# Token and channel mixer: the products of chunks 16 to 54 as two lanes of 64 rows, each in its own order

## The chip, the core and the metric

One Trainium2 chip, one core. The metric is device microseconds of one execution. Engines in the views: PE is TensorE's matmuls, PEld its weight loads, DVE is VectorE, ACT is ScalarE, POOL is GpSimd, SP is SyncE.

## What is computed

```python
w = softmax(weight_gen)                      # (8, 4096, 8 heads, 7 taps), over the taps
x = causal_taps(w, x)                        # out[s] = sum_k w[s,k] * x[s-6+k], per head; (8, 4096, 192)
xt = x.transpose(0, 2, 1)
h = np.maximum(xt @ w_tok1, 0.0) @ w_tok2    # 4096 -> 256 -> 4096: over the sequence
u = x + h.transpose(0, 2, 1)
h2 = np.maximum(u @ w_ch1, 0.0) @ w_ch2      # 192 -> 1536 -> 192: over the channels
return u + h2
```

## The kernel before

The 8 x 4096 positions are 64 chunks of 512 (`NG` = 64, `NCH` = 8 a batch). Each operand of a product is held as a high and a low part, and a product is taken as two or three products of parts. Per chunk `g` the kernel does:

- the attention of a later chunk: tap products and sums on DVE (L278, L292), added into `xa` by DMA, cut into `xh` (L329 on ACT, L332 on DVE), turned and kept (L354), with a softmax for two chunks at a time (L237 to L246);
- token 1 of a later chunk (L600, L602): 8 pairs of products, 384 and 192 columns, into `th`, which ACT seeds from `h1s` (L593) and copies back (L610). From batch 2 on (chunk 16) in parts;
- token 2 of chunk `g + 1` (L643): ten products of 512 columns into `up`, a two-bank PSUM tile that ACT first seeds with a copy of `xb` (L637). Then `uf` (L650 to L655) and its parts `u_hi`, `u_lo` (L678 to L693), here the "u chain";
- channel 1 (L749): six pairs `p` of hidden blocks, each nine steps of two products; the two use rows 0 to 63 and 64 to 127 of PE and write the two banks of one tile `ph`. Then `h`: its high part is ACT's ReLU (L755), its low part DVE's difference (L756). Four `h` are kept (`HB` = 4), so pairs 4 and 5 stay in PSUM until channel 2 has used up a buffer;
- channel 2 (L767): 60 products of full height (128 rows) into two banks `acc`, seeded from `uf` (L816); then `store` (L825 to L847) transposes them on DVE, ACT copies them to `out_tile`, SP stores.

PSUM has eight banks: two for `acc`, three two-bank tiles (tag `w`, a ring in order of use) for `ph`, `up` and `th`. Each engine works through its own list in order. The lists are written in the program's order; where work of the attention, the u chain and the stores stands in DVE's and ACT's lists is chosen by `pump` from planned times (`at`, `on`). PE's list before is plain: channel 1's 108 products, token 2's ten, half of channel 2, token 1, the other half of channel 2.

Of the kernel before, what the change touches and what calls it, by code (L numbers as in the profile page):

```python
# [22 lines left out]
def mixer_kernel(ctx: ExitStack, tc: tile.TileContext, x, wg, wt1, wt2, wc1, wc2, out):  # L23
# [558 lines left out]

    def token1(m):
        b, i = divmod(m, NCH)
        w = w1t.pop(m)
        th = ps_w.tile([P, 2, 512], F32, tag="w", name="th")
        cols = slice(0, D if b < F1 else 2 * D)
        if i == 0:  # L590
            h1s[b] = late.tile([P, KR, 2 * D], F32, tag="h1s", name="h1s")[:, :, cols]
        else:
            nc.scalar.copy(th[:, :, cols], h1s[b])  # L593
        yield
        if b >= F1:
            xh = xht.pop(m)
            for r in range(KR):
                for c in range(CT):
                    rs = slice(r * P, (r + 1) * P)
                    nc.tensor.matmul(th[:, r, 0:2 * D], w[:, c, 0, rs], xh[:, c, :], start=i + c == 0, stop=False,  # L600
                                     skip_group_check=True)
                    nc.tensor.matmul(th[:, r, 0:D], w[:, c, 1, rs], xh[:, c, 0:D], start=False, stop=c == CT - 1,  # L602
                                     skip_group_check=True)
# [19 lines left out]

    ut, uft = {}, {}

    def token2(m, up=None):

        xb, h1, w = xbt.pop(m), h1t[m // NCH], w2t.pop(m)
        seeded = up is None
        if seeded:  # L630
            up = ps_w.tile([P, 2, 512], F32, tag="w", name="up")
            if m < 2:
                nc.scalar.copy(up, xb)
            elif m < FT:
# [104 lines left out]
    def channel1(g, p):  # L739

        u_hi, u_lo = ut[g]
        ph = ps_w.tile([P, 2, 512], F32, tag="w", name="ph")
        steps = [(w, u, k) for w, u in ((w1_hi, u_hi), (w1_lo, u_hi), (w1_hi, u_lo)) for k in range(3)]
        if g == 0:
            steps = [(w, u_hi, k) for k in (2, 0, 1) for w in (w1_hi, w1_lo)] + [(w1_hi, u_lo, k) for k in (0, 2, 1)]
        for n, (w, u, k) in enumerate(steps):
            for j in range(2):
                rows = slice(j * DC, (j + 1) * DC)
                nc.tensor.matmul(ph[:, j, :], w[rows, k, p * P:(p + 1) * P], u[rows, k], start=n == 0,  # L749
                                 stop=n == len(steps) - 1)  # L750
# [9 lines left out]
    def channel2(g, p):  # L760
        acc = acc_t[g]
        h = ht.pop((g, p))
        for j in range(2):
            f = 2 * p + j
            for n, steps in ((1, ((C_HL, 0), (C_HL, 1))), (0, ((A_HI, 0), (A_LO, 0), (A_HI, 1)))):
                for i, (d, l) in enumerate(steps):
                    nc.tensor.matmul(acc[n], w2s[:, f, d], h[:, j, l, :], start=False,  # L767
                                     stop=f == NF - 1 and i == len(steps) - 1, skip_group_check=True)

    def last_chunk(g, p0):  # L770

# [114 lines left out]
    def on(engine, cost, *after):  # L886
        at[engine] = max(at[engine], *after, 0.0) + cost
        return at[engine] + HOP

    class Chain:  # L890
# [4 lines left out]
        def next(self):  # L895
            self.item = next(self.items, None)
# [77 lines left out]

# [64 lines left out]
    with tc.tile_pool(name="pro", bufs=1) as pro, \  # L1039
# [353 lines left out]
```

## Time and profile before

| | us |
|---|---|
| median of 3 runs (2054.68 to 2054.95) | 2054.75 |
| span of the profiled execution, first to last instruction | 2052.6 |
| PE busy in the span | 2031.9 (99%) |
| DVE busy | 1498.8 (73%) |
| ACT busy | 1436.9 (70%) |
| stretch of chunks 16 to 54 (39 chunks) | 585.5 to 1790.0 |

The span is one execution; the runs' times hold 2.15 us outside of it. A matmul's end is modelled (its row is longer than the step from start to start), so the pace of PE is read from the starts.

### The profile page before, as it was taken

How to read it: one execution, taken by the hardware profiler on the slowest of the kernel's cores; microseconds unless marked ns; L12 is line 12 of the kernel's file. 1: busy time of each engine (PE TensorE's matmuls, PEld its weight loads, DVE VectorE, ACT ScalarE, POOL GpSimd, SP SyncE). 2: the span in 40 equal slices, each digit the busy share in tenths (PEclk: the TensorE clock that was granted, in tenths of full speed). 3: DMA queues.
4: the chain of work that ended last, by engine and by line, in shares of the span. 5: the costliest groups of instructions: out<-in, count | busy, mean ns of one | idle time of the engine just before them, and what ended most of it. 6: DMA issues, size and time to landing. Idle time of an engine off the chain costs nothing.

```text
span 2052.6 us, 32256 instructions
## 1 busy us (share of the span) xinstructions
PE 2031.9 (99%) x12831; PEld 1675.4 (82%) x12831; DVE 1498.8 (73%) x1735; ACT 1436.9 (70%) x2282; POOL 210.2 (10%) x292
## 2 busy tenths in 40 slices
PE   7999999999999999999999999999999999999999
PEld 7878888888888888888888888888888888888887
DVE  9899988888987778767777768768678774434343
ACT  7887667677776676676676676676676676676665
POOL 1101111111111101001101111001111010000000
PEclk9999999999999999999999999999999999999999
DMA  9978778887886676666666676766676662222121
GB/s 336 282 226 227 201 212 226 217 223 206 245 212 179 169 192 184 176 201 157 186 197 163 174 200 166 200 177 166 177 200 168 177 181 82 90 73 64 45 65 24
DMA packets 180898, 361.47 MB, mean 176 GB/s; under 512 B 26138, under 2 KB 129178, under 8 KB 165004
## 3 DMA queue, kind: packets, MB, share of 16 engines
q1 hardware_dynamic: 145420, 225.35, 35.5%
q0 software_dynamic: 35328, 134.07, 27.7%
q8 instruction: 100, 1.64, 0.3%
q14 instruction: 50, 0.41, 0.1%
HBM read 222.77 MB, written 70.52 MB: 143 GB/s over the span
## 4 chain that ended last, share of the span: by engine, by line
PE 97%; DVE 2%; ACT 1%; issue 0%; DMA 0%; ACTq 0%; DVEq 0%
PE acc L767 41%; PE ph L749 39%; PE up L643 8%; PE th L600 4%; PE th L602 2%; PE th L621 2%; DVE prk L404 1%; PE up L767 1%; PE tapsum L414 1%; PE acc L786 0%; DVE val L202 0%; PE up L724 0%; PE acc_end L786 0%; ACT few L206 0%; PE turn L414 0%
## 5 line engine op out<-in xcount | busy, mean ns | idle before, releaser
L767 PE MATMUL acc<-h,w2s 128*128 128x512 f32 x3740 | 870.3, 390 | 0.0
L767 PEld LDWEIGHTS acc<-h,w2s 128*128 128x128 f32 x3740 | 698.0, 188 | 143.3 <-issue 0.7
L755 ACT ACTIVATE h<-ph 128x1024 fp32r<-128x1024 f32 x384 | 394.2, 1026 | 365.5 <-PE ph L749 324.6
L756 DVE SCALAR_TENSOR_TENSOR h<-ph,h 128x1024 fp32r<-128x1024 f32 x384 | 467.1, 1218 | 103.8 <-ACT h L755 102.6
L749 PE MATMUL ph<-u_hi,w_hi 64*128 64x512 f32 x2304 | 334.0, 393 | 0.0
L749 PE MATMUL ph<-u_hi,w_lo 64*128 64x512 f32 x2304 | 326.4, 386 | 0.0
L749 PE MATMUL ph<-u_lo,w_hi 64*128 64x512 f32 x2304 | 325.0, 387 | 0.0
L278 DVE TENSOR_TENSOR pr<-xc,wg 128x768 f32<-128x768 f32 x336 | 313.0, 948 | 0.6
L296 POOL DMA_DIRECT2D xa<-pr x168 | 146.5, 872 | 1356.1 <-DVE pr L292 888.5
L749 PEld LDWEIGHTS ph<-u_hi,w_hi 64*128 64x128 f32 x2304 | 211.2, 184 | 63.8 <-issue 20.1
L749 PEld LDWEIGHTS ph<-u_hi,w_lo 64*128 64x128 f32 x2304 | 215.9, 184 | 46.7
L749 PEld LDWEIGHTS ph<-u_lo,w_hi 64*128 64x128 f32 x2304 | 215.9, 184 | 46.4 <-ACT u_lo L737 0.3
L835 ACT COPY out_tile<-oa 32x256 f32<-32x256 f32 x504 | 203.5, 404 | 8.2
L332 DVE TENSOR_TENSOR xh<-xa,xh 128x768 fp32r<-128x768 f32 x48 | 45.8, 955 | 179.3 <-ACT xh L329 179.1
L292 DVE TENSOR_TENSOR pr<-pr 128x768 f32<-128x768 f32 x168 | 159.9, 952 | 3.1
L643 PE MATMUL up<-w,h 128*128 128x512 f32 x630 | 161.2, 402 | 0.0
L655 DVE TENSOR_TENSOR uf<-up,uf 64x512 f32<-64x512 f32 x63 | 43.0, 683 | 145.3 <-ACT uf L651 145.3
L643 PEld LDWEIGHTS up<-w,h 128*128 128x128 f32 x630 | 114.1, 188 | 41.2 <-issue 16.9
L600 PE MATMUL th<-xh,w 128*128 128x384 f32 x384 | 112.4, 358 | 0.0
L835 ACT COPY out_tile<-oc 32x256 f32<-32x256 f32 x252 | 101.6, 403 | 4.5
L637 ACT COPY up<-xb 128x1024 f32<-128x1024 f32 x56 | 57.0, 1018 | 63.4 <-DVE h L756 63.4
L602 PE MATMUL th<-xh,w 128*128 128x192 f32 x384 | 96.2, 250 | 0.0
(115 smaller groups left out, 1728.1 us busy)
## 6 DMA issues: line engine op xcount, KB each, us to landing
w<-s SPq DMA_DIRECT2D x96, 1024.0 KB, 5.8
xa<-pr POOLq DMA_DIRECT2D x168, 384.0 KB, 4.6
xc<-in_x_dram POOLq DMA_DIRECT2D x42, 960.0 KB, 6.8
out_dram<-out_tile SPq DMA_DIRECT2D x128, 192.0 KB, 4.2
xb<-xs SPq DMA_DIRECT2D x348, 64.0 KB, 5.5
xs<-t SPq DMA_DIRECT2D x56, 384.0 KB, 5.4
raw<-in_moe_w_tok_dram SPq DMA_DIRECT2D x16, 1024.0 KB, 8.1
xc<-in_x_dram POOLq DMA_DIRECT2D x12, 840.0 KB, 7.7
```

The costliest lines, as they stand in the source:

```text
L278: nc.vector.tensor_mul(t.rearrange("p t (h g) -> p (t h) g", h=H).rearrange("p (o n) g -> p o n g", o=1), x_k, w)
L292: nc.vector.tensor_add(tap_sums[m], tap_sums[m], tap_prs.pop(m))
L296: nc.gpsimd.dma_start(xat[m].rearrange("p t d -> p (t d)"), tap_sums[m].rearrange("p t d -> p (t d)"), accum_op=ALU.add)
L600: nc.tensor.matmul(th[:, r, 0:2 * D], w[:, c, 0, rs], xh[:, c, :], start=i + c == 0, stop=False, skip_group_check=True)
L602: nc.tensor.matmul(th[:, r, 0:D], w[:, c, 1, rs], xh[:, c, 0:D], start=False, stop=c == CT - 1, skip_group_check=True)
L637: nc.scalar.copy(up.rearrange("p k (n b c) -> p (k n) c b", c=W, b=Q), xb.rearrange("p k (n c b) -> p (k n) c b", c=W, b=Q))
L643: nc.tensor.matmul(up[:, n, :], h1[:, k, d], w[:, l, k * N:(k + 1) * N], start=k == 0 and j == 0 and not seeded, stop=k == KR - 1 and j == ...
L749: nc.tensor.matmul(ph[:, j, :], w[rows, k, p * P:(p + 1) * P], u[rows, k], start=n == 0, stop=n == len(steps) - 1)
L755: nc.scalar.activation(h[:, :, 0, :], ph, AF.Relu)
L756: nc.vector.scalar_tensor_tensor(h[:, :, 1, :], ph, 0.0, h[:, :, 0, :].bitcast(F32), op0=ALU.max, op1=ALU.subtract)
L767: nc.tensor.matmul(acc[n], w2s[:, f, d], h[:, j, l, :], start=False, stop=f == NF - 1 and i == len(steps) - 1, skip_group_check=True)
L835: nc.scalar.copy(dst, src[to:to + Q].rearrange("p (n e d) -> p n e d", n=2, d=Q)[:, n])
```

## The change

From chunk 16 to 54 every product of PE is cut into two of 64 rows: lane 0 has rows 0 to 63, lane 1 rows 64 to 127. Each lane has a list of its own, and `run_lanes` merges the two into PE's one list by planned starts (a slot of 226.7 ns; 170 and 108 for token 1's halves). The two lanes don't write one bank at a time: while lane 0 sums its half of `acc[0]`, lane 1 sums its half of `acc[1]`, and then they swap. A bank goes over by an empty step on DVE or ACT (a `nop`) that waits for the last product of the one lane and for which the first of the other waits. All six `h` of a chunk are taken at once: pairs 4 and 5 into four spare tiles, one block at a time (`take_h_apart`). Token 2 and token 1 move behind the start of channel 2. Chunk 16 holds two token-1 products, and chunk 55, which had one, none; otherwise the program outside of these chunks is as before. A lane's list in a chunk is: lane 0 `ph` (54), `acc[0]` (36), `up` (10), `acc[1]` (24), `th` (8 pairs); lane 1 `ph` (54), `acc[1]` (4), `up` (10), `acc[1]` (20), `th` (8 pairs), `acc[0]` (36).

```diff
+    SLOT, T1_HI, T1_LO = 226.7, 170.0, 108.0
@@ token1 (token2 likewise, with up[:, n, :] and SLOT)
+        if lists is not None:
+            xh = xht.pop(m)
+            for s, rows in enumerate(HALVES):
+                for r in range(KR):
+                    for c in range(CT):
+                        rs = slice(r * P, (r + 1) * P)
+                        lists[s] += [
+                            (T1_HI, ("th", r, m), product(th[:, r, 0:2 * D], w[rows, c, 0, rs], xh[rows, c, :],
+                                                       s == first and i + c == 0)),
+                            (T1_LO, ("th", r, m), product(th[:, r, 0:D], w[rows, c, 1, rs], xh[rows, c, 0:D],
+                                                       stop=c == CT - 1))]
...
+    def take_h_apart(g, p, ph):
+
+        for j in range(2):
+            h = spare[(p - HB) * 2 + j]
+            nc.scalar.activation(h[:, 0, :], ph[:, j, :], AF.Relu)
+            nc.vector.scalar_tensor_tensor(
+                h[:, 1, :], ph[:, j, :], 0.0, h[:, 0, :].bitcast(F32), op0=ALU.max, op1=ALU.subtract
+            )
...
+    def run_lanes(until):
+
+        while True:
+            starts = [lane_start(s) for s in range(2)]
+            if until():
+                return
+            s = min((t, s) for s, t in enumerate(starts) if t is not None)[1]
+            cost, bank, fn = lanes[s].popleft()
+            ins = fn()
+            lane_at[s] = starts[s] + cost
+            if bank is not None:
+                if owner.setdefault(bank, s) != s:
+                    if bank in turn:
+                        behind(ins, turn.pop(bank)[0])
+                        owner[bank] = s
+                else:
+                    count[bank] = count.get(bank, 0) + 1
+                    if count[bank] == ITEMS[bank[:2]]:
+                        by, eng = min((("dve", nc.vector), ("act", nc.scalar)), key=lambda x: at[x[0]])
+                        relay = eng.nop(nofuse=True)
+                        behind(relay, ins)
+                        turn[bank] = relay, on(by, 60, lane_at[s] + HOP)
...
+        def take(p):
+            end = lane_at[1] + HOP
+            (take_h if p < HB else take_h_apart)(g, p, phs.pop(p))
+            extra = 0 if p < HB else 200
+            w_at.append(on("dve", LOW + extra, on("act", TOP + extra, end)))
+            if p == HB - 2:
+                seed(g)
...
+            if p == NP - 2:
+                begin()
...
+        def begin():
...
+            box["two"] = token2(g + 1, lists=box["t2"])
+            next(box["two"])
+            box["two_at"] = max(on("act", 1050, w_at.popleft()), h1_at[(g + 1) // NCH])
...
+            elif box["late"]:
+                upper = a + u + [hook(end_two), *c, late[0], hook(lambda: end_one("late"))]
+                lower = lc[:4] + lu + lc[4:14] + [hook(lambda: seed_late(1))] + lc[14:] + [late[1]] + la
...
+    def in_lanes(g):
+
+        return 2 * NCH <= g < NG - NCH - 1 and (ring or state["token1"] >= g + NCH - 1 and state["done"] > g + NCH)
```

In the changed kernel all products of the lanes carry one line, L469 (`product`), and the tiles of the ring are called `w`. The other lines move: the ReLU of a whole pair L755 is L799, its low part L756 is L800, ReLU and low part of one block are L792 and L793, the copy into `up` L637 is L664, the copies of `out_tile` L835 are L897, the `acc` seeds L816 are L878.

PE's list at the end of channel 1, before: the last steps of `ph`, token 2, the first of channel 2.

```order
L749 MATMUL ph<-u_hi,w_hi 128x512 x5
L749 MATMUL ph<-u_hi,w_lo 128x512 x6
L749 MATMUL ph<-u_lo,w_hi 128x512 x6
L643 MATMUL up<-w_7383,h_5848 128x512 [waits DMAHW0_49,Activation_49]
L643 MATMUL up<-w_7383,h_5848 128x512 x9
L767 MATMUL acc_7589<-h,w2s 128x512 x2
L767 MATMUL acc_7588<-h,w2s 128x512 x3
```

The same place in chunk 24 of the changed kernel. Here `w_5981` is `ph` of the last pair (lane 1), `acc0` is lane 0, `acc1` lane 1, and `w_5982` is `up` (lane 1).

```order
L469 MATMUL w_5981<-u_lo_9048,w1_hi_71 128x512
L469 MATMUL acc0_9256<-h_9202,w2s_73 128x512
L469 MATMUL acc1_9257<-h_9202,w2s_73 128x512 [waits Activation_49]
L469 MATMUL acc0_9256<-h_9227,w2s_73 128x512
L469 MATMUL acc1_9257<-h_9202,w2s_73 128x512
L469 MATMUL acc0_9256<-h_9227,w2s_73 128x512
L469 MATMUL acc1_9257<-h_9202,w2s_73 128x512
L469 MATMUL acc0_9256<-h_9227,w2s_73 128x512
L469 MATMUL acc1_9257<-h_9202,w2s_73 128x512
L469 MATMUL acc0_9256<-h_9227,w2s_73 128x512
L469 MATMUL w_5982<-w2_9049,h1_8770 128x512 [waits DMAHW7_49,DVE_49,Activation_49]
L469 MATMUL acc0_9256<-h_9227,w2s_73 128x512
```

Token 2 stood directly behind channel 1 at full height; now its first product, in lane 1, stands four products of `acc1` behind the lane's last `ph`, alternating with lane 0's `acc0`, which began six products earlier.

ACT's list from the third ReLU of a chunk to the copy into `up`, before:

```order
L755 ACTIVATE h<-ph 128x2x512 [waits PE_49]
L816 COPY acc_11876<-uf 128x512
L816 COPY acc_11877<-uf 128x512
L755 ACTIVATE h<-ph 128x2x512 [waits PE_49,Activation_49]
L637 COPY up<-xb 128x4x8x32 [waits DMAHW2_49,DMAHW3_49,DMAHW1_49,DMAHW4_49,DMAHW0_49,DVE_49]
L835 COPY out_tile<-oa 32x8x32 x2
```

The same stretch in chunk 24 of the changed kernel:

```order
L799 ACTIVATE h<-w 128x2x512 [waits PE_49]
L878 COPY acc_9256<-uf 128x512
L878 COPY acc_9257<-uf 128x512
L799 ACTIVATE h<-w 128x2x512 [waits DVE_49,PE_49]
L792 ACTIVATE h_spare<-w 128x512 [waits DVE_49,PE_49]
L792 ACTIVATE h_spare<-w 128x512 [waits DVE_49]
L664 COPY w<-xb 128x4x8x32 [waits DMAHW5_49,DMAHW6_49,DMAHW2_49,DMAHW7_49,DMAHW1_49,DMAHW0_49]
L792 ACTIVATE h_spare<-w 128x512 [waits PE_49]
L792 ACTIVATE h_spare<-w 128x512 [waits DVE_49]
```

The copy into `up` (`L664`) stood behind the fourth ReLU; now the two ReLUs of the fifth pair stand between, and the second of them waits for the count that DVE's low part of the first block (L793) brings.

DVE's list in chunk 24 of the changed kernel, from the sum of `oc` to the low parts of the fifth pair:

```order
L890 TENSOR_TENSOR oc<-oc 64x512 [waits DVE_49]
L240 TENSOR_REDUCE mx<-wg 128x64 [waits Activation_49]
L800 SCALAR_TENSOR_TENSOR h<-w,h 128x2x512 [waits Activation_49]
L243 TENSOR_SCALAR mx<-mx 128x64 [waits DVE_49]
L244 RECIPROCAL mx<-mx 128x64 [waits DVE_49]
L800 SCALAR_TENSOR_TENSOR h<-w,h 128x2x512 [waits Activation_49]
L246 TENSOR_TENSOR wg<-wg,mx 128x448 [waits DVE_49]
L800 SCALAR_TENSOR_TENSOR h<-w,h 128x2x512 [waits Activation_49]
L278 TENSOR_TENSOR pr<-xc,wg 128x768
L800 SCALAR_TENSOR_TENSOR h<-w,h 128x2x512 [waits Activation_49]
L354 STREAM_TRANSPOSE t<-xa 128x768 [waits DMAHW6_49,DMASW0_49]
L793 SCALAR_TENSOR_TENSOR h_spare<-w,h_spare 128x512 [waits Activation_49] x2
```

Ahead of these rows stand the two transposes of the chunk before and `xh` (L887, L888, L332). One operation of the attention stands between the fourth low part and the first of the fifth pair in chunks 17 to 51 (in odd chunks L292). The softmax rows (L240 to L246) are in the even chunks 18 to 48.

## Rows read from the trace of the kernel before

**Rows 1.** The head of the page: the span.

```profile
span 2052.6 us, 32256 instructions
```

**Rows 2.** Who PE waited for in the whole span: engine, its line, the releaser; us in total, times, longest.

```profile
PE tapsum L414 <- DVE prk L404: 13.1, 5, 9.1
PE th L621 <- ACT xa L461: 2.2, 3, 0.9
PE up L767 <- DVE w2s L561: 0.3, 1, 0.3
```

**Rows 3.** Busy time in the stretch of chunks 16 to 54: us; PE, PEld, DVE, ACT, POOL busy (instructions), granted clock, DMA share, GB/s.

```profile
585.50:1790.00 1204.50, 1204.50 (x7567) 989.63 (x7566) 871.55 (x1022) 835.15 (x1342) 126.64 (x169) 1.00 0.64 174
```

**Rows 4.** Timeline of PE in chunk 30 and the ends of its neighbours: start, us to the end of the last of them, line, operation, count.

```profile
1015.76 2.20 PE L767 MATMUL acc<-h,w2s 128*128 128x512 f32 x9
1017.89 0.97 PE L749 MATMUL ph<-u_hi,w_hi 64*128 64x512 f32 x6
...
1020.09 0.85 PE L749 MATMUL ph<-u_hi,w_hi 64*128 64x512 f32 x6
...
1026.21 0.84 PE L749 MATMUL ph<-u_hi,w_hi 64*128 64x512 f32 x6
...
1029.61 0.84 PE L749 MATMUL ph<-u_lo,w_hi 64*128 64x512 f32 x6
1030.38 2.58 PE L643 MATMUL up<-w,h 128*128 128x512 f32 x10
1032.80 6.96 PE L767 MATMUL acc<-h,w2s 128*128 128x512 f32 x30
1039.60 0.33 PE L600 MATMUL th<-xh,w 128*128 128x384 f32 x1
...
1039.86 0.36 PE L600 MATMUL th<-xh,w 128*128 128x384 f32 x1
1040.06 0.25 PE L602 MATMUL th<-xh,w 128*128 128x192 f32 x1
1040.15 0.36 PE L600 MATMUL th<-xh,w 128*128 128x384 f32 x1
```

**Rows 5.** Timeline of PE in chunk 55, where token 2 stands between the halves of channel 2.

```profile
1804.87 7.00 PE L767 MATMUL acc<-h,w2s 128*128 128x512 f32 x30
1811.70 2.43 PE L643 MATMUL up<-w,h 128*128 128x512 f32 x10
1813.97 6.96 PE L767 MATMUL acc<-h,w2s 128*128 128x512 f32 x30
```

**Rows 6.** Timeline of DVE in channel 1 of chunk 30; in brackets the idle time ahead and what ended it.

```profile
1018.00 0.72 DVE L825 STREAM_TRANSPOSE oa<-acc 128x512 f32<-128x512 f32 x1
1018.64 0.67 DVE L826 STREAM_TRANSPOSE oc<-acc 128x512 f32<-128x512 f32 x1
1019.35 0.69 DVE L828 TENSOR_TENSOR oc<-oc 64x512 f32<-64x512 f32 x1
1020.07 0.96 DVE L292 TENSOR_TENSOR pr<-pr 128x768 f32<-128x768 f32 x1
1020.95 0.61 DVE L237 TENSOR_REDUCE mx<-wg 128x64 f32<-128x448 f32 x1
1021.48 1.22 DVE L756 SCALAR_TENSOR_TENSOR h<-ph,h 128x1024 fp32r<-128x1024 f32 x1
...
1027.53 1.22 DVE L756 SCALAR_TENSOR_TENSOR h<-ph,h 128x1024 fp32r<-128x1024 f32 x1 [0.31 <-ACT h L755]
1028.67 0.95 DVE L292 TENSOR_TENSOR pr<-pr 128x768 f32<-128x768 f32 x1
1029.54 1.82 DVE L278 TENSOR_TENSOR pr<-xc,wg 128x768 f32<-128x768 f32 x2
```

**Rows 7.** Timeline of ACT in the same stretch: the first ReLU and the copy into `up`.

```profile
1020.29 1.03 ACT L755 ACTIVATE h<-ph 128x1024 fp32r<-128x1024 f32 x1 [5.93 <-PE ph L749]
...
1028.79 1.02 ACT L637 COPY up<-xb 128x1024 f32<-128x1024 f32 x1 [1.29 <-DVE h L756]
```

**Rows 8.** Groups of ACT by line and shape, 580 to 1728 us: count | busy us, mean ns of one | idle us before.

```profile
L755 ACT ACTIVATE h<-ph 128x1024 fp32r<-128x1024 f32 x222 | 227.9, 1027 | 217.7 <-PE ph L749 194.7 <-PE acc L767 22.1
...
L637 ACT COPY up<-xb 128x1024 f32<-128x1024 f32 x37 | 37.6, 1017 | 44.1 <-DVE h L756 44.1
...
L593 ACT COPY th<-h1s 128x768 f32<-128x768 f32 x32 | 25.7, 802 | 5.4 <-DVE h L756 5.2
...
L691 ACT CAST u_hi<-uf 64x512 fp32r<-64x512 f32 x38 | 23.5, 619 | 0.6
...
L651 ACT COPY uf<-up 128x512 f32<-128x512 f32 x38 | 22.3, 587 | 0.4
```

**Rows 9.** Groups of DVE by line and shape, the same stretch.

```profile
L756 DVE SCALAR_TENSOR_TENSOR h<-ph,h 128x1024 fp32r<-128x1024 f32 x222 | 269.9, 1218 | 30.0 <-ACT h L755 29.0
...
L681 DVE TENSOR_TENSOR u_lo<-uf,u_hi 128x512 fp32r<-128x512 f32 x38 | 25.7, 676 | 0.0
```

**Rows 10.** Timeline around the one wait of PE behind 100 us: DVE's operation that it waited for, PE's first product after it, and the next products.

```profile
111.84 0.43 DVE L561 TENSOR_TENSOR w2s<-val,w2s 128x256 fp32r<-128x256 f32 x1
112.32 0.72 PE L767 MATMUL up<-h,w2s 128*128 128x512 f32 x2 [0.26 <-DVE w2s L561]
112.66 0.86 PE L767 MATMUL up<-h,w2s 128*128 128x512 f32 x3
```

More of the change, by code (lines that the diff above doesn't have):

```diff
@@ L461, in turn_back, with product, w_tile @@
         nc.scalar.copy(new_xa(m).rearrange("p c d -> p (c d)"), ps[:, 0:NB * P])
+    HALVES = (LO, HI)
+    SLOT, T1_HI, T1_LO = 226.7, 170.0, 108.0
+    def product(to, w, v, start=False, stop=False):
+        return lambda: nc.tensor.matmul(to, w, v, start=start, stop=stop, skip_group_check=True)
+    ring = deque()
+    def w_tile(name):
+        if not ring:
+            return ps_w.tile([P, 2, 512], F32, tag="w", name=name)
+        ring.rotate(-1)
+        return ring[-1]
     w1t, w2t, rawt = {}, {}, {}
@@ L580, in make_h1, with token1 @@
                                            op0=ALU.max, op1=ALU.subtract)
-    def token1(m):
+    def token1(m, lists=None, first=1):
         b, i = divmod(m, NCH)
         w = w1t.pop(m)
-        th = ps_w.tile([P, 2, 512], F32, tag="w", name="th")
+        th = w_tile("th")
         cols = slice(0, D if b < F1 else 2 * D)
@@ L594, in token1 @@
         yield
-        if b >= F1:
+        if lists is not None:
[9 more added lines that the diff above has]
+                                                       stop=c == CT - 1))]
+        elif b >= F1:
             xh = xht.pop(m)
@@ L624, in mixer_kernel, with token2 @@
     ut, uft = {}, {}
-    def token2(m, up=None):
+    def token2(m, up=None, lists=None):
         xb, h1, w = xbt.pop(m), h1t[m // NCH], w2t.pop(m)
@@ L630, in token2 @@
         if seeded:
-            up = ps_w.tile([P, 2, 512], F32, tag="w", name="up")
+            up = w_tile("up")
             if m < 2:
@@ L642, in token2 @@
                 for j, (d, l) in enumerate(steps):
+                    if lists is not None:
+                        for s, rows in enumerate(HALVES):
+                            lists[s].append((SLOT, ("up", n, m), product(
+                                up[:, n, :], h1[rows, k, d], w[rows, l, k * N:(k + 1) * N],
+                                stop=k == KR - 1 and j == len(steps) - 1)))
+                        continue
                     nc.tensor.matmul(up[:, n, :], h1[:, k, d], w[:, l, k * N:(k + 1) * N],
@@ L741, in channel1 @@
         u_hi, u_lo = ut[g]
-        ph = ps_w.tile([P, 2, 512], F32, tag="w", name="ph")
+        ph = w_tile("ph")
         steps = [(w, u, k) for w, u in ((w1_hi, u_hi), (w1_lo, u_hi), (w1_hi, u_lo)) for k in range(3)]
@@ L751, in channel1 @@
         return ph
+    spare = []
+    def take_h_apart(g, p, ph):
[5 more added lines that the diff above has]
+            )
     def take_h(g, p, ph):
@@ L768, in channel2, with lanes_channel1, lanes_channel2 @@
                                      stop=f == NF - 1 and i == len(steps) - 1, skip_group_check=True)
+    def lanes_channel1(g, p, ph):
+        u_hi, u_lo = ut[g]
+        steps = [(w, u, k) for w, u in ((w1_hi, u_hi), (w1_lo, u_hi), (w1_hi, u_lo)) for k in range(3)]
+        return [[(SLOT, None, product(ph[:, s, :], w[rows, k, p * P:(p + 1) * P], u[rows, k], n == 0,
+                                      n == len(steps) - 1)) for n, (w, u, k) in enumerate(steps)]
+                for s, rows in enumerate(HALVES)]
+    def lanes_channel2(g, p):
+        h = [ht[g, p][:, j] if (g, p) in ht else spare[(p - HB) * 2 + j] for j in range(2)]
+        parts = []
+        for n, steps in ((0, ((A_HI, 0), (A_LO, 0), (A_HI, 1))), (1, ((C_HL, 0), (C_HL, 1)))):
+            parts.append([[(SLOT, ("acc", n, g), product(acc_t[g][n], w2s[rows, 2 * p + j, d], h[j][rows, l, :],
+                                                      stop=p == NP - 1 and j == 1 and i == len(steps) - 1))
+                           for j in range(2) for i, (d, l) in enumerate(steps)] for rows in HALVES])
+        return parts
     def last_chunk(g, p0):
         acc = acc_t.pop(g)
-        other = ps_w.tile([P, 2, 512], F32, tag="w", name="acc_end")[:, 0, :]
+        other = w_tile("acc_end")[:, 0, :]
         nc.scalar.copy(other[:, N // 2:], acc[0][:, N // 2:])
@@ L969, in first_h @@
     def first_h():
-        return max(at["pe"] + state["rest"], w_at[0]) + PAIR
+        return max([at["pe"] + state["rest"], *islice(w_at, 1)]) + PAIR
     def next_lo():
@@ L979, in mixer_kernel @@
     MOVES = 2
+    LANE_TIGHT = 600
+    HANDOVER = 60
     state = {"token1": NCH - 1, "token2": -1, "vals": 0, "few": 0, "few_t": 0, "late": False, "jobs": deque(),
              "summed": NCH - 1, "turned": FT - 1, "parts": NCH - 1, "kept": FT - 1, "stored": -1, "out": -1,
-             "done": NCH - 1, "w1": NCH + 1, "channel1": 0, "rest": 0}
+             "done": NCH - 1, "w1": NCH + 1, "channel1": 0, "rest": 0, "open": 0}
     def raw_free(tag):
@@ L1279, in run_picked, with behind @@
         picked.clear()
-    for g in range(NG):
+    lanes, lane_at = [deque(), deque()], [0.0, 0.0]
+    owner, turn, count = {}, {}, {}
+    ITEMS = {("up", 0): 3 * KR, ("up", 1): 2 * KR, ("acc", 0): 3 * NF, ("acc", 1): 2 * NF}
+    SYNC = mybir.DependencyInfo(mybir.DependencyClass.Sync, mybir.DependencyReason.DATA)
+    def behind(ins, of):
+        tc.add_manual_dep(ins.ins, of.ins.name, SYNC, reason="a bank goes to the other half of the rows")
+    ITEMS.update({("th", r): 2 * CT for r in range(KR)})
@@ new lines, in lane_start @@
+    def lane_start(s):
+        while lanes[s] and lanes[s][0][0] == 0:
+            at["pe"] = max(at["pe"], lane_at[s]) if s == 0 else at["pe"]
+            lanes[s].popleft()[2]()
+        if not lanes[s]:
+            return None
+        bank, t = lanes[s][0][1], lane_at[s]
+        if bank in owner and owner[bank] != s:
+            if bank not in turn:
+                return None
+            t = max(t, turn[bank][1] + HANDOVER)
+        return t
+    def run_lanes(until):
[19 more added lines that the diff above has]
+                        turn[bank] = relay, on(by, 60, lane_at[s] + HOP)
+            if s == 0:
+                at["pe"] = lane_at[0]
@@ new lines, in not_before, with between @@
+    def not_before(s, t):
+        lane_at[s] = max(lane_at[s], t)
+    def between(t):
+        state["rest"] = PAIR
+        h = t + PAIR
+        pump(max(at["act"], h + HOP) + TOP + HOP + LANE_TIGHT, (("x", state["token1"] + 1),), h)
+    def in_lanes(g):
+        return 2 * NCH <= g < NG - NCH - 1 and (ring or state["token1"] >= g + NCH - 1 and state["done"] > g + NCH)
+    for g in range(NG):
+        if in_lanes(g):
+            if not ring:
+                spare += [p1.tile([P, 2, N], F32R, tag="val", name="h_spare", bufs=4) for _ in range(4)]
+                ring.extend([ps_w.tile([P, 2, 512], F32, tag="w", name="w") for _ in range(3)])
+                lane_at[:] = [at["pe"]] * 2
+            chunk_in_lanes(g)
+            continue
+        if lanes[1]:
+            run_lanes(lambda: not lanes[1])
+            at["pe"] = max(at["pe"], lane_at[1])
+            need(lambda: g in ut)
```

119 lines of the change are left out of this document (added).

## Prediction

> **What bounds the kernel now.** I read the span first [rows 1], then what the tensor engine (PE) waited for: three kinds of wait, 15.6 us, all in the opening [rows 2]. Over chunks 16 to 54 (585.5 to 1790.0 us, 39 chunks of 30.88 us) PE is busy all 1204.5 us, VectorE (DVE) 872 and ScalarE (ACT) 835, at full granted clock [rows 3]. So PE is the path there, and only the pace of its products counts. The timeline gives it [rows 4]: 27 pairs of 64-row halves of `ph` take 6.12 us (1020.09 to 1026.21), 0.2267 a pair; 30 full-height `acc` products take 6.80 (1032.80 to 1039.60), 0.2267 each. Two halves side by side and one full product thus cost the same "slot". A chunk has 54 + 60 + 10 slots (28.11 us) and one token-1 product: 8 pairs of 0.20 + 0.09, about 2.28. That makes 30.39; about 0.5 us of each chunk is something else.
>
> **The gain: no changes of height.** That 0.5 stands where PE goes from full height to halves and back [rows 4]. Nine `acc` from 1015.76 should end at 1017.80; `ph` begins 1017.89: 0.09. The first nine pairs take 2.20 instead of 2.04: 0.16. The last three pairs from 1029.61 end at 1030.29; `up` begins 1030.38: 0.09. Ten `up` take 2.42 instead of 2.27: 0.15. Together 0.49 a chunk. In chunk 55 `up` follows `acc`, with no change of height, and takes 2.27 after a gap of 0.03 [rows 5]; so I take the whole 0.49, not only the 0.40 without the slower products behind the first. The change keeps halves from chunk 16 through 54; of 78 changes 77 go: 38.5 x 0.49 = **-18.9 us** (bounds -15 and -19). The Trainium skill, "TensorEngine Tiling (Array Packing)", Tiling Modes, Key Properties, says that changing the tiling mode drains TensorE; by it the gaps go with the change of mode, as rows 4 and 5 have it, which bears on rival 3.
>
> The number of slots stays: each lane (lane 0 the lower rows, lane 1 the upper) has 54 + 60 + 10 products and 8 token-1 pairs, at 0.2267 as `ph` shows. I price them as before.
>
> **A new wait: the seed of `up`.** Lane 1 runs six slots behind lane 0. Behind its share of the fifth pair (p = 4), which ends at time E, it has nine slots of the sixth pair and four of `acc1`, and then takes `up`: at E + 13 x 0.2267 = E + 2.95. That product waits for ACT's copy of `xb` into `up`, and on ACT this copy now stands behind both ReLUs of p = 4, the second of which waits for DVE's first low half. From rows:
> - ACT starts a ReLU 0.20 after the last slot (1020.09 to 1020.29) [rows 4, 7]. The half-size ReLU I take as 0.59, the 512-column PSUM copy [rows 8]: done E + 0.79.
> - DVE is not free by then. In order it has the low half of p = 3, one operation of the attention, then this one. Just this sequence stands in the trace: the pair p = 3 ended at 1026.21, its low half began 1027.53, the next operation 1028.67, the one behind 1029.54 [rows 4, 6]: 3.33 behind the pair's end. The fourth pair ends 2.04 before E, so DVE takes p = 4 at E + 1.29; a 512-column half costs about 0.68 [rows 9]: E + 1.97.
> - Second ReLU after a hop of 0.04 (DVE's 1027.53 + 1.22 to ACT's 1028.79 [rows 6, 7]): to E + 2.60. The `up` copy, 0.02 behind it and 1.02 long [rows 8]: E + 3.64. PE started 0.05 after the operation that it waited for (111.84 + 0.43 to 112.32): E + 3.69.
>
> Late by 0.74. And PE's first product after a wait took 0.34 instead of 0.23 (112.32 to 112.66) [rows 10]: 0.11 more. PE's list is one queue, so lane 0 stops too; and lane 1, full to the brim, would not catch up even if it didn't. 0.85 in each of chunks 17 to 51 (35): 29.8. In chunks 52 to 54 the attention is over, DVE is free, and the same sum gives 0.27 + 0.11: 1.1. **+30.9 us** (bounds: 38 x 0.27 = 10, and 38 x 1.0 = 38 where DVE falls one hop further back). The Trainium skill, "PSUM — Partial Sum Buffer", Terms, forbids two engines on one bank at once, reads included; by it such a wait between ACT and DVE on one tile isn't idle caution, though here the two touch different banks. No run here shows a collision.
>
> **A second wait: `ph` of p = 3 in softmax chunks.** With a ring of three tiles it needs the low half of p = 0. Lane 1 ends the former chunk's `acc0` 1.36 into the chunk; DVE starts its two transposes 0.20 later (1017.80 to 1018.00), then has 0.64 + 0.71 + 0.72 for `oa`, `oc` and their sum, 0.88 for `xh`, 0.53 for the softmax sum [rows 6]: it is free at 5.04, ends the low half at 6.26, PE could go at 6.31; lane 0 is there after 27 slots, 6.12. Late 0.19, with restart 0.30, in the 16 even chunks 18 to 48: **+4.8 us** (0 to 8). In odd chunks there's no softmax sum, and ACT's own chain (1.36 + 2.04 + 0.20 + 1.03 + 0.03 + 1.22 + 0.05 = 5.93) is in time by 0.19.
>
> **Entry and exit.** Chunk 16 runs two token-1 products. The second one's seed stands on ACT behind the ten copies of the u chain (2 x 0.59, 8 x 0.62 [rows 8]), whose last waits for DVE behind four attention operations: from the end of `up` 0.20 + 1.18, 0.68 on DVE, then 4 x 0.87 + 0.60 + 0.68, on ACT 0.62 + 0.80, and 0.05: 8.3; lane 0 needs it after 24 slots, 5.44. 2.9 + 0.11 = 3.0. At the exit lane 1 ends its six slots alone: 1.4. **+4.4** (3 to 6).
>
> **At nothing.** The split ReLUs and low halves of two pairs add 2 x (2 x 0.59 - 1.03) = 0.30 on ACT and 2 x (2 x 0.68 - 1.22) = 0.28 on DVE a chunk; both have some 9 us a chunk free [rows 3]; what isn't hidden is in the waits above. The u chain now has 5.44 + 2.28 = 7.7 us from the end of `up` to the next `ph` and needs about 6.9; its low parts are wanted six slots later still: 2 us of cover; past it, each 0.1 costs 0.1 a chunk. The empty steps stand in DVE's and ACT's queues and hold what is behind them until PE ends a bank, but the other lane comes at least 1.3 us later, against 0.25 for the two hops. Behind the seed of `up` the next that is late is that of token 1: on ACT two ReLUs, eight copies and 0.80 end near E + 9.8; lane 1 needs it at E + 3.80 + 30 slots, 10.6: 0.8 of cover. Loads and stores stay the same in number and are issued at the same events; weights are wanted some 20 us after their issue.
>
> **Sum**, on the profiled execution: 2052.6 - 18.9 + 30.9 + 4.8 + 4.4 = 2073.8, and 2.15 outside the span, as 2054.75, the median, has it: **2076 us**. A chunk would go from 30.88 to about 31.2 (odd) and 31.5 (even).
>
> **Rivals.**
> 1. Faster: the seed of `up` is in time. It decides at one place: if the second ReLU did not queue behind DVE, the copy would end at E + 0.20 + 2 x 0.59 + 1.04 = 2.42, half a microsecond early. For it speaks that before the change this copy had 0.57 to spare (ends 1029.81, `up` 1030.38) [rows 4, 7]; against it the wait that stands in ACT's list. 2054.75 - 18.9 + 4.8 + 4.4 = **2045**. Break-even is a stall of 0.26 a chunk.
> 2. The lanes mesh badly. The list was laid out for token-1 halves of 170 and 108 ns; rows 4 show 0.20 and 0.09. In one queue each of 16 may hold the other lane by up to 0.025: 0.4 a chunk, 15 us: **2084 to 2091**. Against: the sum of a pair is near (0.28 to 0.29).
> 3. The change doesn't do what it says: gaps at `ph` and `up` belong to waits, not to height. Then nothing is won: **2095**. Against: rows 5, where `up` waits for the same things without a gap.
>
> **Chances.** Forecast 0.60, rival 1 0.20, rival 2 0.12, rival 3 0.08. The forecast's own range, with the low and the high ends of its terms in part together, is 2055 to 2089; with half of rival 1 and most of rival 2: **2045 to 2092**, which leaves out about 0.17. A measurement of this kernel tells 0.2% (4.1 us) from no change: faster 0.19 (rival 1), same 0.07 (stalls about half my size), slower 0.74.
>
> **What would show it.** Even slots of 0.2267 with no gap at `ph` and `up` (the gain); a wait of PE for the copy into `up`, 0.6 to 0.9 each in 38 chunks, some 28 us in all (the loss); one of about 0.2 for the low half of `h` in every second chunk; one of 3 us in chunk 16. Wrong it would be if that first wait is missing or below 0.3, or if slots in the lanes aren't 0.2267.

## The result, and the profile after

The changed kernel takes 2068.69 us against 2054.77 for the kernel before, in runs side by side: 1.0068 times, 95% interval 1.0053 to 1.0082. It is slower by 13.9 us, where 21 were forecast. The head of the page, and the rows of all token-2 products on PE and on the weight loader (busy us, mean ns; idle us ahead of them and what ended it), which answer to [rows 1]:

```profile
span 2066.9 us, 39312 instructions
...
L469 PE MATMUL w<-w,h 64*128 64x512 f32 x780 | 194.9, 393 | 11.0 <-ACT w L664 11.0
...
L469 PEld LDWEIGHTS w<-w,h 64*128 64x128 f32 x780 | 140.7, 184 | 40.3 <-ACT w L664 26.9
```

What PE waited for in the whole span (us in total, times, longest), against [rows 2]; L664 is the copy of `xb` into `up`, L1389 the empty step. Below it, what ACT waited for at the ReLUs of pairs 4 and 5 in chunks 16 to 54:

```profile
PE tapsum L414 <- DVE prk L404: 13.6, 6, 9.2
PE w L469 <- ACT w L664: 11.0, 35, 0.4
...
PE w L676 <- ACT w L664: 0.8, 1, 0.8
PE w L469 <- ACTq L1389: 0.4, 1, 0.4
...
PE w L469 <- ACT w L609: 0.2, 1, 0.2
```

```profile
ACT h_spare L792 <- DVE h_spare L793: 75.4, 78, 1.4
```

The wait that the prediction names is there, 35 times, and so is its cause, once in each of 78 pairs. Busy time in the same 39 chunks, which now take from 585.6 to 1804.9 (columns as in [rows 3]):

```profile
585.60:1804.90 1219.30, 1207.77 (x10949) 1053.85 (x10949) 875.00 (x1100) 848.92 (x1422) 126.87 (x169) 1.00 0.64 172
```

1204.5 have become 1219.3, at the same granted clock; VectorE and ScalarE have hardly more work. Chunk by chunk, from the first `ph` of one to that of the next, in us (one later kernel beside it, in which only the stall at `up` is gone):

| chunks | before | after | after - before | `up_8`, below |
|---|---|---|---|---|
| 0 to 15 | 497.90 | 497.89 | 0 | 497.85 |
| 16 (one token 1 more: 2.28) | 30.89 | 35.57 | +4.69 | 35.53 |
| 17 to 51 | 1080.95 | 1091.20 | +10.25 | 1065.48 |
| 52 to 54 | 92.66 | 92.59 | -0.07 | 91.48 |
| 55 (one token 1 less) | 30.84 | 30.17 | -0.67 | 30.17 |

**The stall, in chunk 24.** PE, from lane 1's first `ph` product of the sixth pair to the restart:

```profile
851.18 0.39 PE L469 MATMUL w<-u_hi,w_hi 64*128 64x512 f32 x1
...
851.86 0.39 PE L469 MATMUL w<-u_hi,w_lo 64*128 64x512 f32 x1
852.08 0.39 PE L469 MATMUL acc<-h,w2s 64*128 64x512 f32 x1
852.09 0.39 PE L469 MATMUL w<-u_hi,w_lo 64*128 64x512 f32 x1
...
853.21 1.29 PE L469 MATMUL acc<-h,w2s 64*128 64x512 f32 x9
854.73 0.50 PE L469 MATMUL w<-w,h 64*128 64x512 f32 x1 [0.23 <-ACT w L664]
854.73 0.50 PE L469 MATMUL acc<-h,w2s 64*128 64x512 f32 x1
855.06 0.39 PE L469 MATMUL w<-w,h 64*128 64x512 f32 x1
```

ACT and DVE at the same time:

```profile
851.37 0.60 ACT L792 ACTIVATE h_spare<-w 128x512 fp32r<-128x512 f32 x1 [0.97 <-PE w L469]
853.16 0.60 ACT L792 ACTIVATE h_spare<-w 128x512 fp32r<-128x512 f32 x1 [1.19 <-DVE h_spare L793]
853.65 1.02 ACT L664 COPY w<-xb 128x1024 f32<-128x1024 f32 x1
```

```profile
851.58 0.97 DVE L354 STREAM_TRANSPOSE t<-xa 128x768 f32<-128x768 f32 x1
852.47 0.65 DVE L793 SCALAR_TENSOR_TENSOR h_spare<-w,h_spare 128x512 fp32r<-128x512 f32 x1
853.79 0.69 DVE L793 SCALAR_TENSOR_TENSOR h_spare<-w,h_spare 128x512 fp32r<-128x512 f32 x1 [0.67 <-ACT h_spare L792]
```

Lane 1 begins its sixth pair at 851.18: that is E. First ReLU at E + 0.19, DVE's low half at E + 1.29 because an attention step is ahead of it, second ReLU at E + 1.98, the copy from 2.47 to 3.49, PE at 3.55. The product was due after 13 slots, at 2.95. The rows also show the gain: lane 0 goes from `ph` to `acc` at 852.08 without a gap.

The wait view shows 0.23 here, and 11.0 us over 35 chunks. In truth lane 1 starts 0.60 late, and the first slot after it takes 0.33 instead of 0.227 (854.73 to 855.06). A row's length is longer than a slot, so most of the stall hides under rows that seem to be still running. The Trainium skill, "Perfetto Trace Analysis", Per-engine timelines (Tensor Engine Instruction), says that a matmul's end is an estimate, not a measurement; these rows agree. The weight loader's idle time for the same releaser, 26.9 us, is the better figure: it comes to what the stall turns out to cost, and follows it again in `up_2` below.

### The profile page after: what moved, and what is told of

It reads as the page before. It is cut to its first block, busy times and chain, and to the rows that moved or that the text cites. A ratio compares the mean times of both kernels' runs of the same rounds, so it can differ in the third digit from the quotient of the medians.

```text
span 2066.9 us, 39312 instructions
## 1 busy us (share of the span) xinstructions
PE 2033.7 (98%) x16201; PEld 1737.9 (84%) x16201; DVE 1501.7 (73%) x1813; ACT 1449.3 (70%) x2360; POOL 210.6 (10%) x292
## 4 chain that ended last, share of the span: by engine, by line
PE 79%; DVE 14%; ACT 5%; issue 2%; ACTq 0%; DMA 0%; DVEq 0%
PE acc L469 22%; PE w L469 21%; PE acc L811 15%; PE ph L782 10%; DVE h L800 5%; PE w L782 5%; DVE pr L278 2%; PE up L676 2%; ACT h L799 2%; ACT w L664 2%; PE th L648 2%; DVE pr L292 1%; DVE prk L404 1%; DVE h_spare L793 1%; PE w L676 1%
## 5 line engine op out<-in xcount | busy, mean ns | idle before, releaser
L469 PE MATMUL acc<-h,w2s 64*128 64x512 f32 x3120 | 556.5, 388 | 0.0
L469 PEld LDWEIGHTS acc<-h,w2s 64*128 64x128 f32 x3120 | 441.3, 184 | 34.6
L469 PE MATMUL w<-u_hi,w_hi 64*128 64x512 f32 x1404 | 370.9, 389 | 0.0
L469 PE MATMUL w<-u_hi,w_lo 64*128 64x512 f32 x1404 | 368.7, 387 | 0.0
L469 PE MATMUL w<-u_lo,w_hi 64*128 64x512 f32 x1404 | 368.4, 386 | 0.0
L469 PE MATMUL acc<-h_spare,w2s 64*128 64x512 f32 x1560 | 335.6, 386 | 0.0
L811 PE MATMUL acc<-h,w2s 128*128 128x512 f32 x1400 | 325.6, 390 | 0.0
L799 ACT ACTIVATE h<-w 128x1024 fp32r<-128x1024 f32 x210 | 215.6, 1027 | 148.7 <-PE w L469 80.8
L278 DVE TENSOR_TENSOR pr<-xc,wg 128x768 f32<-128x768 f32 x336 | 313.0, 945 | 0.2
L811 PEld LDWEIGHTS acc<-h,w2s 128*128 128x128 f32 x1400 | 261.8, 188 | 54.4 <-issue 0.7
L800 DVE SCALAR_TENSOR_TENSOR h<-w,h 128x1024 fp32r<-128x1024 f32 x210 | 255.7, 1218 | 71.0 <-ACT h L799 70.5
L469 PEld LDWEIGHTS acc<-h_spare,w2s 64*128 64x128 f32 x1560 | 258.4, 184 | 23.4
L469 PEld LDWEIGHTS w<-u_hi,w_hi 64*128 64x128 f32 x1404 | 250.8, 184 | 24.1 <-DVE h L800 2.9
L469 PEld LDWEIGHTS w<-u_hi,w_lo 64*128 64x128 f32 x1404 | 253.8, 184 | 20.0
L469 PEld LDWEIGHTS w<-u_lo,w_hi 64*128 64x128 f32 x1404 | 254.9, 184 | 17.0
L897 ACT COPY out_tile<-oa 32x256 f32<-32x256 f32 x504 | 203.7, 404 | 7.6
L469 PE MATMUL w<-w,h 64*128 64x512 f32 x780 | 194.9, 393 | 11.0 <-ACT w L664 11.0
L469 PEld LDWEIGHTS w<-xh,w 64*128 64x128 f32 x1280 | 187.6, 186 | 6.6 <-ACTq L1389 0.8
L469 PE MATMUL w<-xh,w 64*128 64x384 f32 (+1 forms) x1280 | 192.2, 300 | 0.6 <-ACTq L1389 0.4
L469 PEld LDWEIGHTS w<-w,h 64*128 64x128 f32 x780 | 140.7, 184 | 40.3 <-ACT w L664 26.9
```

The lines of the kernel that those rows point to most:

```text
L278: nc.vector.tensor_mul(t.rearrange("p t (h g) -> p (t h) g", h=H).rearrange("p (o n) g -> p o n g", o=1), x_k, w)
L469: return lambda: nc.tensor.matmul(to, w, v, start=start, stop=stop, skip_group_check=True)
L799: nc.scalar.activation(h[:, :, 0, :], ph, AF.Relu)
L800: nc.vector.scalar_tensor_tensor(h[:, :, 1, :], ph, 0.0, h[:, :, 0, :].bitcast(F32), op0=ALU.max, op1=ALU.subtract)
L897: nc.scalar.copy(dst, src[to:to + Q].rearrange("p (n e d) -> p n e d", n=2, d=Q)[:, n])
```

## Experiments

None of these kernels leaves out part of the computation. `relus_first` to `sum_later` ran beside each other (before: 2054.70), and so did the last three (before: 2054.82).

**`relus_first`: the wait taken out of ACT's list.** Both ReLUs of a pair ahead of both low halves; no engine gets more or less work.

```diff
-        for j in range(2):
-            h = spare[(p - HB) * 2 + j]
-            nc.scalar.activation(h[:, 0, :], ph[:, j, :], AF.Relu)
+        hs = [spare[(p - HB) * 2 + j] for j in range(2)]
+        for j, h in enumerate(hs): nc.scalar.activation(h[:, 0, :], ph[:, j, :], AF.Relu)
+        for j, h in enumerate(hs):
             nc.vector.scalar_tensor_tensor(
```

> Both ReLUs of a pair taken apart stand ahead of both its low halves, so that the second ReLU no longer waits for VectorE, and the copy into `up` behind it doesn't either. Theory A, the stall at `up` comes from that wait: the copy would start some 1.3 us behind the pair's end and end at 2.35, ahead of its use at 2.95; TensorE's wait for the copy goes from every chunk. Odd chunks from 31.18 to about 30.46, even ones, which keep the wait at the fourth `ph`, from 31.2 to 30.7: 2047 us (2045 to 2050). Rival B, the copy is late because ScalarE or VectorE has too much to do at that place: the stall shrinks by less than half or comes back at the seed of token 1: 2060 or more. Rival C, halves don't save the gaps at a change of height: even without this stall the time stays above the 2054.8 of the kernel before.

Measured: 2042.31 us, 0.9936 of the kernel before (0.9924 to 0.9949). Odd chunks take 30.40, even ones 30.48. PE has no wait for L664 in the lanes any more. ACT's rows for the same pair, and PE's first token-2 product:

```profile
845.48 1.09 ACT L791 ACTIVATE h_spare<-w 128x512 fp32r<-128x512 f32 x2 [0.96 <-PE w L469]
846.45 1.03 ACT L664 COPY w<-xb 128x1024 f32<-128x1024 f32 x1
```

```profile
848.22 0.39 PE L469 MATMUL w<-w,h 64*128 64x512 f32 x1
```

The copy ends at 847.48, 0.74 before its use. So theory A holds, B and C fall: the engines have room, and without this one wait the halves beat the kernel before. It came out 5 us faster than I expected, mostly since the wait at the fourth `ph` nearly went too: even chunks came to 30.48, not 30.7 (see `sum_later`). The profiled execution, from which the rows come, took 2041.04.

**`up_8` and `up_2`: the wait stays, its cover changes.** Lane 1 takes token 2 behind eight, or two, products of `acc1` instead of four; lists of ACT and DVE as in the changed kernel.

```diff
-                lower = lc[:4] + lu + lc[4:14] + [hook(lambda: seed_late(1))] + lc[14:] + [late[1]] + la
+                lower = lc[:8] + lu + lc[8:14] + [hook(lambda: seed_late(1))] + lc[14:] + [late[1]] + la
```

> Lane 1 takes token 2 behind eight products of `acc1` instead of four; ACT's and VectorE's lists stay, the second ReLU still waits for VectorE. The products come 0.91 us later, the copy into `up` came 0.61 late in the trace: theory A says 0.3 in time, no wait for it, and the same time as with both ReLUs first, 2047 us (2045 to 2050), since lane 0, not lane 1, ends `up`. Rival B (engines too full there): the work behind the copy is late now, at the seed of token 1 in lane 1 or in the u chain, and the time stays at 2060 or more.

> Lane 1 takes token 2 behind two products of `acc1` instead of four: the same copy is waited for 0.45 us longer in each of 38 chunks. Theory A: 2068.7 + 38 x 0.45 = 2086 us (2083 to 2088), with one wait of about 1 us a chunk. If another wait ends last there (rival B), less than half of it: 2069 to 2077.

Measured: `up_8` 2041.84 us (0.9936, 0.9924 to 0.9949), `up_2` 2085.87 (1.015, 1.0136 to 1.0164). PE's wait in `up_2`:

```profile
PE w L469 <- ACT w L664: 28.1, 38, 0.9
```

The weight loader's row for the same wait there, 17.3 us more than in the changed kernel, where the runs are 17.2 us longer:

```profile
L469 PEld LDWEIGHTS w<-w,h 64*128 64x128 f32 x780 | 140.7, 184 | 57.6 <-ACT w L664 44.2
```

The first cut of the u chain (once a chunk; first and last start in one stretch) in the changed kernel, `relus_first`, `up_8` and `up_2`:

```profile
L711 ACT CAST u_hi<-uf x33: 622/622/624, 677.5 to 1675.0; 128x512 fp32r<-128x512 f32 x33
```

```profile
L711 ACT CAST u_hi<-uf x34: 620/622/623, 675.6 to 1679.6; 128x512 fp32r<-128x512 f32 x34
```

```profile
L711 ACT CAST u_hi<-uf x34: 620/622/625, 676.0 to 1680.3; 128x512 fp32r<-128x512 f32 x34
```

```profile
L711 ACT CAST u_hi<-uf x33: 622/622/624, 678.2 to 1690.2; 128x512 fp32r<-128x512 f32 x33
```

A chunk takes (1675.0 - 677.5) / 32 = 31.17, and in the others 30.42, 30.43 and 31.63. Two slots less cover add 0.46 a chunk, two slots' worth; four more take away the whole stall and no further. `up_2` fell into theory A's range; `up_8`, like `relus_first`, came out below its own, for the same reason. Two edits that have nothing in common but the lateness of this copy against its use give the same time within 1 us. The stall, with all that hangs on it, is worth 2068.7 - 2041.8 = 26.9 us.

**`sum_later`: the softmax sum behind the first low half.** The planner is kept from placing it (L240, which the edit numbers 546) at the end of a chunk.

```diff
+                if ... or state["hold"] and c.item[1] == 546: continue
...
-            between(lane_at[1])
+            state["hold"] = 1; between(lane_at[1]); state["hold"] = 0
```

> In even chunks the softmax sum goes behind VectorE's first low half, so `ph` of the fourth pair no longer waits. If the two stalls of a chunk add up, as my prediction had it, 16 x 0.25 go: 2064.7 us. But in the trace lane 0 alone loses 0.25 there, lane 1 hardly, and lane 0 then waits 0.2 less at `up`: if the two overlap in this way, even chunks go from about 31.2 only to the 31.18 of odd ones: 2068 to 2069.

Measured: 2069.81 us (1.0073, 1.0059 to 1.0086), 1.1 slower than the changed kernel and 0.8 over the higher of the two expectations. Not a clean test: the planner put a tap product (L278, 0.87 us) behind the sum, the second low half came later, and the wait moved from the fourth `ph` to the fifth (0.25 late and 0.11 for the restart). Odd chunks took 31.14, even ones 31.30. Of this wait, even chunks paid 0.16. That the wait at the fourth `ph` adds to the stall at `up` is refuted all the same by odd and even chunks of the changed kernel itself: 31.16 and 31.20. What made the wait at the fourth `ph` shows in `relus_first`, whose DVE list has the sum where the changed kernel has it. DVE from the transposes to the first low half in the changed kernel; PE's first product of the chunk (839.53) and of lane 0's fourth pair (845.82) there; and the same DVE rows and the first product of the chunk in `relus_first`:

```profile
841.12 0.72 DVE L887 STREAM_TRANSPOSE oa<-acc 128x512 f32<-128x512 f32 x1 [0.53 <-PE acc L469]
...
844.55 1.21 DVE L800 SCALAR_TENSOR_TENSOR h<-w,h 128x1024 fp32r<-128x1024 f32 x1
```

```profile
839.53 0.41 PE L469 MATMUL w<-u_hi,w_hi 64*128 64x512 f32 x1
...
845.68 0.39 PE L469 MATMUL w<-u_hi,w_lo 64*128 64x512 f32 x1
845.82 0.49 PE L469 MATMUL w<-u_hi,w_hi 64*128 64x512 f32 x1
```

```profile
833.86 0.41 PE L469 MATMUL w<-u_hi,w_hi 64*128 64x512 f32 x1
```

```profile
835.23 0.72 DVE L887 STREAM_TRANSPOSE oa<-acc 128x512 f32<-128x512 f32 x1 [0.31 <-PE acc L469]
...
838.67 1.21 DVE L800 SCALAR_TENSOR_TENSOR h<-w,h 128x1024 fp32r<-128x1024 f32 x1
```

In the first, counted from the chunk's start at 839.53, the transposes come at 1.59, the low half is done at 6.23, and `ph` starts at 6.29, due at 6.15. In the second, counted from 833.86, it is 1.37 and 6.02, and `ph` starts in time, at 6.15 (only the slot behind its first is 0.05 long). The stall at `up` holds lane 1 longer (0.60) than lane 0 (0.39 to 0.56), so lane 1 ends its `acc0` 1.39 into the next chunk, and 1.16 without the stall. The wait at the fourth `ph` is thus a child of the stall at `up`: lane 0 waits there and then waits less at `up`.

**`both`: `relus_first` and `sum_later` in one.**

> Both ReLUs first and the softmax sum behind the first low half. Without the stall at `up`, even chunks took 30.46, odd ones 30.39. If what is left of the wait at the fourth `ph` is the softmax sum's, even chunks come to 30.39 and the time to 2041.2 us. If the tap product that the planner then puts behind the first low half (0.87 us) makes the fifth `ph` wait, as it did with the sum moved alone (0.25 + 0.11), even chunks go to 30.8 and the time to 2047 us.

Measured: 2045.04 us (0.9949, 0.9936 to 0.9961), even chunks 30.65 and odd ones 30.39 (from chunk 19 on): the second case, in part. DVE's second low half, and PE at the fifth pair:

```profile
841.80 0.95 DVE L278 TENSOR_TENSOR pr<-xc,wg 128x768 f32<-128x768 f32 x1
842.66 1.22 DVE L800 SCALAR_TENSOR_TENSOR h<-w,h 128x1024 fp32r<-128x1024 f32 x1
```

```profile
843.61 0.39 PE L469 MATMUL w<-u_hi,w_lo 64*128 64x512 f32 x1
843.94 0.50 PE L469 MATMUL w<-u_hi,w_hi 64*128 64x512 f32 x1
...
844.27 0.39 PE L469 MATMUL w<-u_hi,w_hi 64*128 64x512 f32 x1
```

The low half ends at 843.88, `ph` follows at 843.94. A slot 0.05 too long was traded for a wait of 0.11 and a restart. In the profiled execution another 1.5 us lie in chunks 16 and 17 (last section).

**`relay_pool`: `relus_first` with the empty steps in GpSimd's list.**

```diff
-                        by, eng = min((("dve", nc.vector), ("act", nc.scalar)), key=lambda x: at[x[0]])
+                        by, eng = "pool", nc.gpsimd
...
-                        turn[bank] = relay, on(by, 60, lane_at[s] + HOP)
+                        turn[bank] = relay, lane_at[s] + HOP + 60
```

> As with both ReLUs first (2042.3 us), and the empty steps that hand a bank over stand in GpSimd's list instead of VectorE's or ScalarE's. If they cost nothing where they stood, as the prediction has it, and the 1.3 us of cover hold on GpSimd too: 2042.3, within 1 us. If they held their engines, even chunks come down by up to 0.07: 2041. If GpSimd's list, in which DMA issues wait for VectorE's tap products, holds the empty steps for longer than 1.3 us, each such time stops TensorE for the rest: by up to 1 us in each of 39 chunks, 2045 to 2080.

Measured: 2046.4 us (0.9958, 0.9946 to 0.9971). PE's new waits:

```profile
PE w L469 <- POOLq L1389: 1.6, 1, 1.6
PE acc L469 <- POOLq L1389: 1.2, 1, 1.2
```

From chunk 18 on nothing changes (30.39 and 30.47): there the steps cost nothing in either list. Only in chunks 16 and 17, with chunk 16's two token-1 products, GpSimd's list is late: 38.35 instead of 34.89, and 31.83 instead of 30.52. What holds its list there was not followed up, and not all of this is the wait itself, since the granted clock fell after it, to 0.72 and then, up to 628, 0.71:

```profile
622.00:625.00 3.00, 2.32 (x20) 2.32 (x22) 2.54 (x3) 2.14 (x6) 1.43 (x2) 0.72 0.56 103
```

**`up_between`: more changes of height, in the kernel before.** Token 2 at full height between the fifth and the sixth pair.

```diff
...
+                if mid and p == HB:
+                    do_token2(*two)
-        picked = list(picks(g, 100, 1))
+        picked = [] if mid else list(picks(g, 100, 1))
```

> The kernel before, with token 2 at full height between the fifth and the sixth pair of channel 1 in 35 of the chunks 16 to 54 (the four at a batch's end stay), so that a chunk changes the height four times instead of twice. If a change costs what the rows of before show (0.09 + 0.16 into halves, 0.09 + 0.15 out of them), 35 x 0.49 = 17 us are added: 2072 us, with gaps of 0.09 on both sides of `up` that no wait explains; the copy into `up` may be late by 0.1 to 0.3 besides (it needs the third pair's tile, free 9.3 us into the chunk, and ends at 10.4, where `up` is wanted at 10.3): up to 2082. If the gaps belong to waits and not to the height (rival 3 of the prediction), the same number of them stays: 2055 us, or what a wait of the copy adds, with no gap at the sixth pair.

Measured: 2102.72 us (1.0231, 1.0217 to 1.0245), 48 us more, beyond both expectations. At least 20.9 of them are a wait that I hadn't foreseen, which falls ahead of the place looked at:

```profile
PE ph L749 <- DVE h L756: 20.9, 35, 1.6
```

PE behind it:

```profile
1047.23 2.59 PE L643 MATMUL up<-w,h 128*128 128x512 f32 x10
1049.75 0.97 PE L749 MATMUL ph<-u_hi,w_hi 64*128 64x512 f32 x6
...
1052.02 7.12 PE L767 MATMUL acc<-h,w2s 128*128 128x512 f32 x30
1058.97 0.33 PE L600 MATMUL th<-xh,w 128*128 128x384 f32 x1
```

From 1047.23 to 1058.97 it takes 11.74 for 10 + 9 + 30 slots, 11.11 at 0.2267: 0.63 more, of which 0.15 is the slow start of `up` that every chunk before had. The two new changes cost 0.48, without a wait: 0.24 each, or 17 of the 48 us. As a time the run decides nothing, because of its own wait, and some 10 us were not traced; its rows carry the price of a change of height.

## Why the prediction was right, and where its terms were off

The forecast case came true: slower, inside its own range of 2055 to 2089, by the mechanism it names. One sign has to be read with care. The prediction asked for a wait of 0.6 to 0.9 in 38 chunks, some 28 us, and called itself wrong below 0.3. The wait view has 0.23 in chunk 24 and 11.0 us in 35 chunks; only the products' starts (0.60 late) and the weight loader (26.9 us) show the wait at its size. Likewise the waits forecast at the fourth `ph` and in chunk 16 hardly show in the view, but do in the starts. Term by term, with chunks 16 to 55 as measure (+14.2 us):

| term | forecast | measured |
|---|---|---|
| no changes of height | -18.9 | -19.2: 39 chunks from 30.88 to 30.39 each (odd chunks of `relus_first`, `up_8`) |
| stall at the seed of `up` | +30.9 | +26.9: changed kernel against `up_8` |
| wait at the fourth `ph` | +4.8 | +0.8 in the changed kernel (31.20 against 31.16), +1.4 in `up_8` |
| entry and exit | +4.4 | about +5: chunk 16 2.9 over its slots, 17 and 18 0.3, 54 0.3, 55 1.6 |

(The stall is taken against `up_8`, so the sum goes with the 1.4 of `up_8`.)

- **The gain** holds to 0.3 us. An odd chunk without stalls takes 30.39, the sum of its slots and one token 1. With that rival 2 is out as well: two lanes in one queue cost nothing for token 1's halves of 0.20 and 0.09. Rival 3 is out by `relus_first`, `up_8` and the rows of `up_between`. The Trainium skill, "TensorEngine Tiling (Array Packing)", Tiling Modes, Key Properties, says that a change of mode drains TensorE; the rows of `up_between` agree, at 0.24 us for each change.
- **The stall at `up`** is the step that was over-sized, by 4.0 us. The prediction's chain E + 0.79, 1.29, 1.97, 2.60, 3.64, 3.69 was measured as 1.29 and 1.98 for DVE and the second ReLU, and then 2.47 and 3.49 for start and end of the copy: I let the copy begin when the ReLU's row ends, but it begins 0.49 after the ReLU's start, though that row is 0.60 long. So 0.60 late instead of 0.74. PE's list does stop both lanes, but lane 0 loses only 0.56 in odd and 0.39 in even chunks. In chunks 52 to 54 the forecast of 1.1 met 1.12.
- **The wait at the fourth `ph`** was there (0.14 late, 0.19 forecast, and 0.11 for the restart). The step that failed was to add it: both waits follow from one lag between the lanes, and the chunk pays for it once. 3.4 us of the 7.3 between forecast and time lie here.
- **Entry and exit** came out near their size, in part by luck. In chunk 16 the step named is there: lane 0 stands from 616.82 to 618.73 for the seed of the second token 1, which ends at 618.68. That is 1.9 us where 2.9 were forecast, since three attention operations stood on DVE ahead of the last cut (613.45, 614.35 and 615.78), not four.

```profile
617.89 0.79 ACT L609 COPY w<-h1s 128x768 f32<-128x768 f32 x1
```

```profile
618.73 0.72 PE L469 MATMUL w<-xh,w 64*128 64x384 f32 x3 [0.21 <-ACT w L609]
```

 Another 0.7 us of the chunk go in `relus_first` (34.89), and with them PE's wait for an empty step in ACT's list (L1389); the prediction had put the empty steps at nothing. At the exit, chunk 55 waits 0.8 us by the view for its own copy into `up`, which the prediction did not have; what lane 1's last slots cost there was not separated.
- **Rival 1** was not the case, but its sum was tested: 2045 forecast, 2041.8 and 2042.3 measured, with the 4.8 that it also counted.

Both `relus_first` and `up_8` beat the kernel before by 0.6%.

## What to carry to other kernels

Before an edit of one engine's list, look at what is queued behind each new wait on the other engines: here two instructions that didn't need each other's result waited in turn on one tile, and an innocent copy behind them cost 27 us. Put instructions of one kind on one tile together, or give the consumer as many slots of cover as the chain is late. And when two stalls come from one lag, price the lag once.

## What the runs showed of the chip that I had not expected

- **ScalarE overlaps neighbours.** Two 512-column ReLUs in a row take 1.09, not 1.20, and the next instruction starts 0.97 behind the first: the step is 0.49, the row 0.60.
- **A lane can stand idle without a wait in the view.** In chunk 16 of the changed kernel lane 0 stands for 1.9 us while lane 1 goes on at 0.2267 a slot; the view gives 0.2 us for L609.
- **The clock can fall behind such a stretch.** In `both`, one lane stood from 616.1 on and both from 617.0 to 618.0, and then the granted clock fell: 0.77 over the next 2 us, and 0.50, the level of 1.2 GHz, over the 2 us after that:

```profile
612.00:618.00 6.00, 5.17 (x43) 4.16 (x39) 5.93 (x9) 5.60 (x10) 0.00 (x0) 1.00 1.04 295
618.00:620.00 2.00, 2.00 (x12) 2.00 (x14) 1.93 (x4) 0.00 (x0) 0.00 (x0) 0.77 1.03 212
620.00:622.00 2.00, 2.00 (x17) 2.00 (x17) 2.00 (x3) 0.25 (x1) 1.34 (x2) 0.50 0.21 63
```

 The profiled execution of `relus_first` has nearly the same idle time in the same place and kept 1.00; chunks 16 and 17 of `both` are 1.5 us longer than there. The times of all executions point to the clock: two of `relus_first` with a mean granted clock of 1.000 took 2040.7 to 2041.0 us and three with 0.998 took 2042.3 to 2042.6; two of `both` with 1.000 took 2043.6 to 2043.8 and three with 0.998 to 0.999 took 2045.0 to 2045.2. Why it fell in some and not in others isn't shown.
